# Loading v through GpSimd's DMA queue with a cast on the way, and running a fixed table of orders: a chunk-selecting attention with a gated feed-forward layer behind it

## The chip, the cores and the metric

The kernel runs on one core of a Trainium2 chip. The metric is the device time of one execution in microseconds (us); below, times without a unit are us. A core has five engines that run their own instruction streams and meet at semaphores: PE (TensorE, matrix multiplication), ACT (ScalarE), DVE (VectorE), POOL (GpSimd) and SP (SyncE, which here only issues DMA transfers). Transfers are issued by SP, ACT or POOL and carried out by the core's DMA engines.

## What is computed

The inputs are q, k and v of shape (4, 8, 768, 64), in float32, and the weights of a gated feed-forward layer. For each query, the keys are taken in chunks of 32; an upper bound of the score of each chunk is made from the chunk's minimum and maximum of k, the six best causal chunks are kept, and an ordinary softmax attention runs over them. Its result goes through an RMS norm and the gated layer.

```python
k_min = np.min(k_chunks, axis=3)
k_max = np.max(k_chunks, axis=3)
ub = np.sum(np.maximum(q[:, :, :, None, :] * k_min[:, :, None, :, :], q[:, :, :, None, :] * k_max[:, :, None, :, :]), axis=-1)
ub = np.where(causal, ub, -1000000000.0)
top_chunks = np.argsort(ub, axis=-1)[..., -top_k:]
scores = scale * np.matmul(q, k.transpose(0, 1, 3, 2))
mask = sel & (pos[:, None] >= pos[None, :])
attn = np.exp(scores)        # masked, less the row's maximum
attn = attn / (np.sum(attn, axis=-1, keepdims=True) + 1e-09)
x = np.matmul(attn, v)       # then (batch, position, head * 64): 3072 x 512
xn = x / rms * rms_g
g = xn @ w_gate              # 512 x 1536
val = xn @ w_val             # 512 x 1536
out = (g * sigmoid(g) * val) @ w_out   # 1536 x 512
```

## The kernel before, in words

The 3072 tokens are cut into twelve blocks of 256 (four batches by three blocks of the sequence), taken in the order of `ORDER` (line 501); block (b, m) is block m of batch b. A name like `scores(2, 1, 0)1` means batch 2, block 1, head group 0 (four heads of eight), against key block 1.

For each block, `load_qk` (line 586) brings k and q in float32, `load_v` (line 614) brings v in two halves of 128 tokens. `job` (line 768) transposes k and q on DVE ("turn"), makes bf16 copies of them on ACT or POOL ("half"), the chunk minima and maxima on DVE ("ext"), their difference ("dk") and operands derived from them ("bd", "KX", "relu", "qx", "qm"). `pick` (line 647) multiplies these on PE ("upper"), selects the best six on DVE and makes a mask. `unit` (line 911) is the scores on PE, followed by an exponential on ACT and, on the diagonal, a triangular cut on POOL ("tri", line 936). `values` (line 991) multiplies with `VX`, which holds v in bf16 and a column of ones behind each head, so that the softmax's denominator comes out of the same multiplication. `norm` (line 1024) makes the normalized, transposed activations `xsT`; for the last eight blocks the transposition is a DMA from SP ("across"). `ffn` (line 1099) has, per block, six pairs of units "wg" and "wv" (the two first weight matrices), tanh on ACT, "tg" on DVE, a copy "vcopy" on ACT, "hh" on POOL or DVE, and then "project" with the third weight matrix, a copy "out" and a store.

v takes this way: SP issues a load of 256 KB (128 tokens, eight heads, float32) into `vraw`, of which there are two; ACT or POOL copies a head group from there into one of the 18 rotating `VX` tiles, and this copy makes the bf16 ("vx", line 901). Each `VX` tile serves all later blocks of its batch.

The weights come in nine transfers (three each of wg, wv and wo), issued by POOL, cast to bf16 on the way; they wait for `dk(0, 0, 0)` (`GATES`, line 508). The k, q and v loads of block 2 wait for a part of wg, those of block 3 for parts of wo (`HELD`, line 584).

The order of the work is no Python loop's. Every step is recorded as an operation with its engine (or several to choose from), its cost, what it reads and writes and which buffers it takes. `Plan.run` (line 255) then simulates the engines and DMA queues (`Rings`, line 37) and picks for each engine, from what is ready, the operation with the earliest of the 1,580 due times in the table `DUE`. Where PE would stand idle before about 60 us, it puts in matmuls whose result is not used (`keep_busy`, line 1242): 77 narrow ones of 128 columns ahead of the first scores, and 39 wide ones of 512 columns in eleven places after that. What is written out is five fixed instruction streams; at run time only semaphores hold them.

## Time and profile before

| what | us |
|---|---|
| three runs | 299.69, 300.06, 302.14 |
| median | 300.06 |
| span of the profiled execution | 297.4 |
| ACT busy in it | 216.7 |
| DVE busy in it | 217.1 |
| POOL busy in it | 155.6 |

The span is the time from the first instruction to the last in one profiled execution; the device time of the runs has a few us around it. The profile gives no separate device time for the profiled execution, so its span stands beside the median of the runs, 2.66 us below it. Busy time counts neither waits nor the issue of DMA transfers. In views of the trace, a line ends with the idle time of the engine just before the instruction, and with what released it.

### The profile page before, as it was taken

Reading aid. Unit: us, or ns where it says so; the run is one execution under the profiler, and the core shown is the slowest. Engines: PE = TensorE matmul, PEld = TensorE weight load, DVE = VectorE, ACT = ScalarE, POOL = GpSimd, SP = SyncE. Lnnn points to the kernel's source line nnn. Section 1 sums busy time; section 2 is a strip of 40 time slices with the busy share of each in tenths; the row PEclk is TensorE's granted clock in tenths of the full one; section 3 lists DMA queues with packets and bytes.
Section 4 is the critical chain, followed back from the end, with each engine's and each line's share of the span. In section 5 each row is a group of like instructions: output and inputs, shape, how many; then the busy total and the mean of one; then the engine's idle time right before and its main releaser. Section 6 shows DMA issues by size and latency. Waiting matters only on the chain.

```text
span 297.4 us, 11418 instructions
## 1 busy us (share of the span) xinstructions
PE 282.5 (95%) x4672; PEld 213.4 (72%) x4672; DVE 217.1 (73%) x623; ACT 216.7 (73%) x372; POOL 155.6 (52%) x266
## 2 busy tenths in 40 slices
PE   7879999999999996999999999899999999999994
PEld 7548777657858854878767787488688778678763
DVE  6987774977998998888999999679356454456430
ACT  4897877688979876987985797677587668565331
POOL 4885858755976864475583276538044114214120
PEclk9999999999999999999999999999999999999998
DMA  7999998755676656654768576511014021011011
GB/s 188 208 204 206 255 197 163 159 130 134 141 194 154 144 136 103 149 100 110 205 135 162 108 193 150 133 40 39 0 57 55 1 82 30 2 73 35 2 71 71
DMA packets 86388, 35.08 MB, mean 118 GB/s; under 512 B 74816, under 2 KB 81728, under 8 KB 86336
## 3 DMA queue, kind: packets, MB, share of 16 engines
q1 hardware_dynamic: 80736, 29.12, 42.6%
q0 software_dynamic: 4752, 4.72, 9.4%
q8 instruction: 36, 0.59, 0.8%
q10 hardware_dynamic: 848, 0.53, 0.7%
q14 instruction: 16, 0.13, 0.2%
HBM read 28.58 MB, written 6.29 MB: 117 GB/s over the span
## 4 chain that ended last, share of the span: by engine, by line
PE 76%; DMA 9%; DVE 4%; ACT 4%; SPq 3%; POOL 1%; issue 1%; DVEq 0%; POOLq 0%; ACTq 0%
PE F L1122 39%; PE F L1169 18%; PE S L922 6%; PE F L998 6%; PE F L680 3%; SPq L528 3%; PE S L933 2%; DMA xsT<-xs 2%; DMA qraw<-in_q_dram 2%; DMA vraw<-in_v_dram 2%; DMA kraw<-in_k_dram 2%; DVE kx L809 1%; POOL hh L1144 1%; DVE m L739 1%; ACT th L1129 1%
## 5 line engine op out<-in xcount | busy, mean ns | idle before, releaser
L972 ACT ACTIVATE pt<-S 128x1024 bf16<-128x1024 f32 (+3 forms) x104 | 85.6, 857 | 19.7 <-PE S L933 18.2
L1144 POOL TENSOR_TENSOR hh<-tg,vs 128x512 bf16<-128x512 bf16 x48 | 55.7, 1164 | 42.6 <-ACT vs L1141 22.9
L1133 DVE SCALAR_TENSOR_TENSOR tg<-th,F 128x512 bf16<-128x512 bf16 x72 | 48.4, 680 | 39.3 <-ACT th L1129 33.7
L1122 PE MATMUL F<-xsT,wg 128*128 128x256 bf16 (+1 forms) x608 | 72.6, 267 | 3.7 <-DVE xnat L1017 1.7
L1122 PE MATMUL F<-xsT,wv 128*128 128x256 bf16 (+1 forms) x608 | 72.4, 267 | 0.6 <-DMA xsT<-xs 0.3
L1169 PE MATMUL F<-wo,hh 128*128 128x512 bf16 (+1 forms) x300 | 68.5, 371 | 1.8 <-POOL hh L1144 0.6
L1122 PEld LDWEIGHTS <-wg 128*128 128x128 bf16 x608 | 55.6, 98 | 13.5 <-issue 2.7
L1122 PEld LDWEIGHTS <-wv 128*128 128x128 bf16 x608 | 55.2, 98 | 9.7 <-DMA vraw<-in_v_dram 0.8
L1129 ACT ACTIVATE th<-F 128x512 bf16<-128x512 f32 x72 | 42.5, 598 | 19.7 <-PE F L1122 17.4
L942 POOL TENSOR_SCALAR_AFFINE_SELECT pt<-pt 128x512 bf16<-128x512 bf16 x48 | 32.2, 674 | 32.3 <-ACT pt L972 31.7
L1169 PEld LDWEIGHTS <-hh 128*128 128x128 bf16 x300 | 27.7, 98 | 28.4 <-issue 1.8
L1141 ACT ACTIVATE vs<-F 128x512 bf16<-128x512 f32 x48 | 28.7, 598 | 13.2 <-PE F L1122 10.1
L922 PE MATMUL S<-qb,kb 32*128 32x256 bf16 (+1 forms) x800 | 32.8, 253 | 2.3 <-ACT qb L801 2.0
L809 DVE TENSOR_REDUCE kx<-kT 128x16 f32<-128x512 f32 x48 | 30.4, 664 | 0.0
L998 PEld LDWEIGHTS <-pt 128*128 128x128 bf16 x672 | 24.8, 98 | 3.1 <-issue 0.3
L998 PE MATMUL F<-VX,pt 128*128 128x65 bf16 x672 | 26.6, 194 | 0.2 <-ACT vs L1141 0.2
L922 PEld LDWEIGHTS <-kb 32*128 32x128 bf16 x800 | 13.9, 92 | 15.0 <-issue 14.4
L933 PE MATMUL S<-mtd,chunkrow 32*128 32x128 bf16 (+2 forms) x384 | 20.5, 203 | 0.2 <-issue 0.2
L933 PE MATMUL S<-mto,chunkrow 32*128 32x128 bf16 (+2 forms) x384 | 19.9, 203 | 0.0
L1017 DVE TENSOR_TENSOR xnat<-F,rden 128x256 bf16<-128x256 f32 x48 | 19.2, 415 | 0.7
L933 PEld LDWEIGHTS <-chunkrow 32*128 32x128 bf16 x768 | 18.5, 93 | 1.2 <-issue 0.4
L1034 ACT ACTIVATE junk<-xnat 128x512 bf16<-128x512 bf16 x24 | 15.1, 631 | 5.4 <-DVE xnat L1017 5.0
(71 smaller groups left out, 337.2 us busy)
## 6 DMA issues: line engine op xcount, KB each, us to landing
vraw<-in_v_dram SPq DMA_DIRECT2D x24, 256.0 KB, 4.4
out_dram<-osb SPq DMA_DIRECT2D x23, 256.0 KB, 2.4
kraw<-in_k_dram SPq DMA_DIRECT2D x72, 64.0 KB, 2.4
qraw<-in_q_dram SPq DMA_DIRECT2D x72, 64.0 KB, 2.2
QX<-qT SPq DMA_DIRECT2D x32, 64.0 KB, 2.7
wg<-in_moe_w_gate_dram POOLq DMA_DIRECT2D x3, 512.0 KB, 12.3
wv<-in_moe_w_val_dram POOLq DMA_DIRECT2D x3, 512.0 KB, 14.3
wo<-in_moe_w_out_dram POOLq DMA_DIRECT2D x3, 512.0 KB, 23.5
```

Of the source, the lines that this page charges most:

```text
L809: plan.op(f"ext{n}{J}", "DVE", 0.585, 0.67, lambda n=n, op=op: VE.tensor_reduce(out=at(kx)[:, g, n], in_=at(kT).rearrange("p h (j c x) -> ...
L922: TE.matmul(s[a // 2][:, a % 2, c0:c0 + q1 - q0], kbt[r, t, ks], qbt[r, t, q0:q1], start=(t == 0), stop=(t == 1 and not mask), skip_group_ ...
L933: TE.matmul(o, chunkrow[r, BLK * kg + P * e:BLK * kg + P * (e + 1)], mv, start=False, stop=(d == 1), skip_group_check=True)
L942: GE.affine_select(out=d, in_=d, compare_op=ALU.is_ge, fill=0.0, base=0, pattern=[[0, 4], [1, P]], channel_multiplier=-1)
L972: lambda pt=pt, hs=hs, c0=c0, c1=c1, x=sc[hp]: SE.activation(out=at(pt)[:, hs, c0:c1], in_=at(x)[:, :, c0:c1], func=ACT.Exp, scale=SCALE), ...
L998: TE.matmul(o[:, a, :], p_[:, a, off:off + P], vt[:, e, a, :], start=(kb_ == 0 and a == 0), stop=(kb_ == nkb - 1 and a == 3), skip_group_c ...
L1122: TE.matmul(at(p_)[:, n * W:(n + 1) * W], w[:, g, ht * P:(ht + 1) * P], at(xT)[:, g, x0:x0 + W], start=(g == 0), stop=(g == NP - 1), skip_ ...
L1129: plan.op(f"tanh{U}.{hp}", "ACT", 0.48, 0.6, lambda th=th, gp=gp: SE.activation(out=at(th), in_=at(gp), func=ACT.Tanh, scale=0.5), pri - 0 ...
L1133: VE.scalar_tensor_tensor(out=at(tg), in0=at(th), scalar=1.0, in1=at(gp), op0=ALU.add, op1=ALU.mult), pri - 30, reads=[th, gp], writes=[tg ...
L1141: plan.op(f"vcopy{U}.{hp}", "ACT", 0.48, 0.6, lambda vs=vs, vp=vp: SE.activation(out=at(vs), in_=at(vp), func=ACT.Copy), pri + 0.1, reads= ...
L1144: plan.op(f"hh{U}.{hp}", "POOL", 1.11, 1.16, lambda tg=tg, vs=vs, hh=hh: GE.tensor_tensor(out=at(hh), in0=at(tg), in1=at(vs), op=ALU.mult) ...
L1169: TE.matmul(at(op)[:, cs], at(key)[:, o:o + P], wo[:, ht, cs], start=(ht == 0), stop=(ht == NHT - 1), skip_group_check=True)
```

## The change

v is now loaded by POOL instead of SP, straight from float32 in memory into bf16 in its place. There is one tile per block, `VX[b, m]`, for all eight heads, so twelve tiles that stay for the whole kernel; `vraw`, the 18 rotating tiles and the 24 copies "vx" are gone. The ones are set in twelve memsets in place of 18. A load waits for its tile's ones, and `values` waits for the loads that it needs.

```diff
-    buffers("vraw", 2, [P, 2, NG, 4, D], FP32)
-    buffers("VX", 18, [P, 2, 4, D + 1], BF16)
+    VX = {(b, m): sb.tile([P, 2, H, D + 1], BF16, name=f"VX{b}{m}") for b in range(B) for m in range(NBLK)}
...
-        for i, t in enumerate(store["VX"]):
+        for i, x in enumerate(ORDER):
...
     def load_v(i):
         b, m = ORDER[i]
-        key = ("vraw", b, m)
         for e in range(2):
             t0 = BLK * m + P * e
-            dma(f"load v{b}{m}{e}", "SP", v[b, :, t0:t0 + P, :].rearrange("a p d -> p a d"),
-                lambda e=e: at(key)[:, e].rearrange("p g a d -> p (g a) d"),
-                64, 0.023 if i < 2 else 0.019, loads_due(i, 2 if i != 1 else -1), writes=[key],
-                takes=[(key, "vraw")] if e == 0 else (),
-                behind=[HELD[i][1]] if i in HELD and e == 0 else ())
+            dma(f"load v{b}{m}{e}", "POOL", v[b, :, t0:t0 + P, :].rearrange("a p d -> p a d"),
+                lambda e=e: VX[b, m][:, e, :, 0:D], 64, 0.023, loads_due(i, 2), writes=[("VX", b, m, e)],
+                reads=[("ones", (b, m))])
...
-        flex(f"vx{J}", {
-            "POOL": (0.57, 0.62, lambda: GE.tensor_copy(vout(), vin())),
-            "ACT": (0.54, 0.63, lambda: SE.activation(out=vout(), in_=vin(), func=ACT.Copy)),
-        }, base + 4 - first, reads=[vraw] + ones, writes=[vx], takes=[(vx, "VX")])
...
-                    p_, vt = at(pts[kg]), at(("VX", b, kg, g))
+                    p_, vt = at(pts[kg]), VX[b, kg]
...
-                        TE.matmul(o[:, a, :], p_[:, a, off:off + P], vt[:, e, a, :],
+                        TE.matmul(o[:, a, :], p_[:, a, off:off + P], vt[:, e, 4 * g + a, :],
```

The second half of the change replaces the planner. `DUE`, `Rings` and the simulation in `run` are gone; a table `STEPS` names each operation (its number times eight, plus the engine) in the order in which it is written out, and a table `SLOTS` says which buffer of its pool each one takes. Negative entries are the unused matmuls.

```diff
+        seen = set()
+        for x in self.STEPS:
+            if x < 0:
+                n, slot = divmod(-x, 16)
+                fill[-1](n // 2, slot, n % 2)
+                continue
+            seq, e = divmod(x, 8)
+            o = self.ops[seq]
+            assert all(d.seq in seen for d in o.deps + o.after), o.name
+            seen.add(seq)
+            o.alts[self.ENGINES[e]][2]()
```

So the order on all engines is new, and with it some choices of engine. What the streams of the two kernels show:

| | before | after |
|---|---|---|
| transfers that SP issues | 262 | 238 |
| v loads that POOL issues | 0 | 24 |
| copies "vx" on ACT, on POOL | 10, 14 | 0, 0 |
| "relu" on POOL, on DVE | 22, 2 | 14, 10 |
| "dk" on POOL, on DVE | 19, 5 | 9, 15 |
| "half" on POOL, on ACT | 26, 22 | 22, 26 |
| operations on DVE | 426 | 450 |
| unused matmuls, narrow and wide | 77 and 39 | 103 and 34 |
| wide ones behind the first wg unit | 11 | 0 |
| changes between kinds of matmul on PE | 121 | 126 |

On POOL the first instructions are now: two memsets of ones and one of BO, the load of half of v of block (0, 0), two memsets, the making of `ident` (the identity matrix that the unused matmuls and DVE's first constants read), two memsets, the other half of (0, 0) and one of (1, 0), a memset, `half k(0, 0, 0)`, the other half of (1, 0), `dk(0, 0, 0)`, a memset, and the first transfer of wg. The eight loads of the blocks that follow stand among POOL's work from its 63rd operation (`load v201`, behind the operands "bd" of block (2, 0) and ahead of an "hh") to its 113th, and the other twelve up to its 194th of 228. On SP, the k and q loads of block (1, 0) now follow those of block (0, 0) directly. The transfers on POOL's queue share eight semaphores in turn: the ninth on the queue (the third part of wg) waits for the first (the first half of v) to have landed, and so on.

More of the change, by code (lines that the diff above doesn't have):

```diff
@@ L607, in load_qk @@
                     takes=[(key, nm + "raw")] if first else (),
-                    behind=[HELD[i][0]] if i in HELD and first else ())
+                    behind=[HELD[i]] if i in HELD and first else ())
                 first = False
@@ L664, in takes, with held @@
             return [(key, pool)] if new else []
+        def held(key):
+            return [] if new else [key]
         def bank():
@@ L1005, in job @@
             o = plan.op(f"values{J}{s}", "PE", 0.129 * nkb, 0.129 * nkb + 0.16, values, pri,
-                        reads=have + [("VX", b, x, g) for x in range(m + 1)],
+                        reads=have + [("VX", b, x, e) for x in range(m + 1) for e in range(2 if x < m else s + 1)],
                         writes=[av], takes=[(av, "F")])
@@ L1245, in keep_busy @@
             TE.matmul(store["F"][slot][:, 0:x.shape[1]], ident[:], x, start=True, stop=True)
-    for o in plan.run(in_order=("kraw", "qraw", "vraw", "kT", "qT", "kb", "qb", "QX", "VX", "xsT", "xs", "hh", "xnat"),
-                      fill=(1.6, 5.6, 60.0, 0.0565, 0.216, "F", keep_busy)):
-        o.fn()
-    kernel.plan = plan
+    plan.run(fill=(1.6, 5.6, 60.0, 0.0565, 0.216, "F", keep_busy))
 _INS = ['q', 'k', 'v', 'moe_w_gate', 'moe_w_val', 'moe_w_out', 'moe_rms_g']
```

276 lines of the change are left out of this document (33 added, 243 removed), and 230 rows, old and new, of tables (DUE, SLOTS, STEPS).

## The prediction

> **What bounds the kernel now.** I read the page first: busy shares and the chain that ended last.
>
> ```profile
> span 297.4 us, 11418 instructions
> PE 282.5 (95%) x4672; PEld 213.4 (72%) x4672; DVE 217.1 (73%) x623; ACT 216.7 (73%) x372; POOL 155.6 (52%) x266
> PE 76%; DMA 9%; DVE 4%; ACT 4%; SPq 3%; POOL 1%; issue 1%; DVEq 0%; POOLq 0%; ACTq 0%
> ```
>
> PE is the bound. The change takes no useful matmul away, so it can win only what PE loses: idle time, and matmuls whose result is not used. The busy time by stretches tells where (start and end, length, then the busy time of PE, PEld, DVE, ACT, POOL, with instructions; granted clock, DMA share, GB/s):
>
> ```profile
> 0.00:20.00 20.00, 16.00 (x271) 11.56 (x272) 16.09 (x45) 14.66 (x25) 14.63 (x56) 1.00 1.00 200
> 20.00:40.00 20.00, 18.41 (x331) 14.78 (x330) 15.68 (x47) 17.56 (x40) 14.65 (x27) 1.00 1.20 221
> 40.00:60.00 20.00, 19.96 (x306) 15.06 (x306) 13.78 (x43) 13.89 (x27) 14.12 (x23) 1.00 0.87 169
> 60.00:80.00 20.00, 18.77 (x273) 14.09 (x273) 16.32 (x50) 17.98 (x37) 12.12 (x19) 1.00 0.52 129
> ...
> 100.00:120.00 20.00, 17.41 (x346) 11.89 (x345) 17.95 (x62) 14.58 (x25) 12.33 (x19) 1.00 0.58 126
> 120.00:140.00 20.00, 19.26 (x380) 16.45 (x377) 16.63 (x51) 16.99 (x29) 12.80 (x18) 1.00 0.55 116
> ...
> 180.00:200.00 20.00, 19.13 (x408) 13.57 (x400) 15.37 (x62) 13.95 (x23) 10.59 (x17) 1.00 0.44 108
> ...
> 280.00:297.40 17.40, 13.56 (x98) 9.28 (x95) 3.86 (x6) 5.05 (x9) 3.46 (x3) 0.96 0.16 60
> ```
>
> Length less busy time is PE's idle time: 4.0 in the first 20 us, 3.8 at the end, and between them 1.59 + 0.04 + 1.23 + 2.59 + 0.74 + 0.87 = 7.06; in the stretches left out PE is busy throughout. Those 7.06 and the unused matmuls are the prize; from 200 to 280 us there is none.
>
> **The start.** The timeline of PE and the chain of waits show it.
>
> ```profile
> 1.71 6.38 PE L1245 MATMUL F<-ident 128*128 128x128 bf16 x77 [1.71 <-POOL eps L551]
> 9.15 0.29 PE L922 MATMUL S<-qb,kb 32*128 32x128 bf16 x8 [1.06 <-ACT qb L801]
> ...
> 19.37 0.29 PE L922 MATMUL S<-qb,kb 32*128 32x128 bf16 x8 [0.95 <-ACT qb L801]
> ...
> 22.27 0.37 PE L698 MATMUL F<-qT,BO 64*64 64x32 f32 x10 [0.45 <-ACT xsT L1087]
> ...
> 22.85 1.07 PE L1122 MATMUL F<-xsT,wg 128*128 128x128 bf16 x16
> ```
>
> ```profile
> 10.83 6.03 DMA qraw<-in_q_dram
> ...
> 22.92 1.00 PE F L1122 x16
> 23.92 0.22 PE S L922 x8
> ...
> 49.72 2.16 PE F L1169 x10
> ```
>
> ```profile
> L1245 PE MATMUL F<-chunkrow,ident x39: 377/379/391, 9.4 to 37.3; 128*128 128x512 bf16 x39
> ```
>
> ```profile
> L1245 PE MATMUL F<-chunkrow,ident x11: 379/379/389, 25.7 to 37.3; 128*128 128x512 bf16 x11
> ```
>
> Dense PE prices come from the chain: 2.16/10 = 0.216 for a matmul of 512 columns, 1.00/16 = 0.0625 for one of 128. The first wg unit starts at 22.9, 13.75 after the first scores (9.15); of that, 28 wide unused matmuls are 6.05 and the two waits shown 1.4. Behind it follow the other 11, 2.4 us. (The second "x" rows are all 39 of them and those behind 22.8.)
>
> **Part by part.**
>
> *ident.* POOL made it by 1.7. In the new stream a load of v (and some memsets, 0.4) stands ahead. Such an issue is not in the trace; the nearest rows are the weights', of 512 runs, where a v load has 1,024:
>
> ```profile
> L528 POOL DMA_DIRECT2D wg<-in_moe_w_gate_dram x3: 767/777/992, 9.8 to 14.2; - x3
> ```
>
> So 0.77 if runs cost nothing, 1.98 if they cost all; I take 1.2. PE then starts at 1.7 + 1.2 + 0.4 = 3.3, and the narrow matmuls take 6.38 and 26 × 0.0625 = 1.6 more: first scores at 11.3, against 9.15. To the first wg unit there are now 34 wide ones (7.3), the same work (13.75 − 6.05 − 1.4 = 6.3) and one score unit more, 0.3 by its row (0.22 and change): 24.9 to 25.2 if nothing else waits. I take 24.9, **+2.0**; bounds +1.5 and +2.8 by the price of the issue. I see no slack to hide it: PE's stream here is one piece, and unused matmuls are work like any other. What goes are the waits for ACT: ACT loses two copies "vx" and hands `half k`, `half q` and a scaling of these two blocks to POOL and DVE. And q of block (1, 0), whose landing at 16.9 stands in the chain, is issued without two v loads ahead.
>
> *Behind it.* The score unit that has moved forward: **−0.3**. No unused matmul is left behind the first wg unit: **−2.4**; this holds only if the weights are there. They are close:
>
> ```profile
> L528 POOL DMA_DIRECT2D wo<-in_moe_w_out_dram x2: 747/802/857, 20.9 to 21.8; - x2
> ...
> DMA to landing us min/median/max: 22.6/23.9/25.2
> ```
>
> The last part lands at 21.8 + 25.2 = 47.0, and the first project (the row at 49.72) needs it: 2.7 of slack. In the new stream PE reaches that place at about 49.72 + 2.0 − 0.3 − 2.4 = 49.0, which leaves 2.0. v of block (2, 0), half a MB which shared the DMA engines until then, now queues behind the weights; at the 200 GB/s and more of those stretches that gives back some 2 us. So about 4 us of cover remain. Five changes of kind more: the 0.22 of a score unit are two rounds of 0.0625 and 0.1 for going in and out, so **+0.3**.
>
> *Casts and SP.*
>
> ```profile
> L904 POOL CAST VX<-vraw 128x512 bf16<-128x512 f32 x14 | 8.5, 618 | 1.8 <-DMA vraw<-in_v_dram 1.8
> L905 ACT ACTIVATE VX<-vraw 128x512 bf16<-128x512 f32 x10 | 6.1, 631 | 0.1
> ```
>
> ```profile
> SPq L528 <- DMA vraw<-in_v_dram: 4.8, 3, 1.8
> ```
>
> ```profile
> L528 SPq DMA_DIRECT2D vraw<-in_v_dram x24: 384/580/1961, 4.1 to 187.0; - x24
> ```
>
> ```profile
> L528 SPq DMA_DIRECT2D vraw<-in_v_dram x2: 427/651/875, 11.3 to 11.8; - x2
> ...
> DMA to landing us min/median/max: 12.2/15.5/18.7
> ```
>
> ACT loses 6.1, POOL 8.5. SP loses 24 × 0.58 = 14 of issuing, and the waits of 4.8 in which it stood behind a slow v load: the second half of v of block (1, 0), issued at 11.8, landed 18.7 later, at 30.5. POOL gains 24 × 1.2 = 29 (bounds 18 and 48) and loses some relu, dk and half to DVE, so it comes to some 60% of the span, less in most stretches than DVE, which gets about 24 small operations more and was busy 18 of 20 around 110 us. Behind each v load on POOL stands an "hh" or "tri" that PE needs two or three units later; that cover is one issue, 1.2, and where it is thin PE waits.
>
> Where SP held PE, the chain says so:
>
> ```profile
> 106.00 0.94 SPq L528
> ...
> 110.23 2.06 DMA QX<-qT
> ...
> 125.74 1.32 SPq L528
> ...
> 128.59 1.74 DMA kraw<-in_k_dram
> ```
>
> The idle 2.59, 0.74 and 0.87 (100 to 140, 180 to 200) end a chain of SP issues, k loads and the transposing or crossing DMAs behind them. With 14 us off SP I let 3.2 of these 4.2 go. The 2.8 of idle in 20 to 80 us hang on ACT, POOL and DVE, whose work is reshuffled; there I let nothing go net: the thin places above cost what the casts bring. **−3.2**; bounds 0 (each stall has a successor) and −6.
>
> Sum: 2.0 − 0.3 − 2.4 + 0.3 − 3.2 = −3.6, span 293.8; with the 2.66 that the median lies above the span, **296.5**.
>
> **The DMA side, and a rule.**
>
> ```profile
> q1 hardware_dynamic: 80736, 29.12, 42.6%
> q0 software_dynamic: 4752, 4.72, 9.4%
> ```
>
> A packet of SP's queue takes 0.426 × 16 × 297.4 / 80736 = 25 ns (361 bytes on average), one of POOL's 0.094 × 16 × 297.4 / 4752 = 94 ns (993 bytes as written). A v packet is 256 bytes read and 128 written; with 64 per engine and load I take 25 ns, the row of its size, and 94 ns as the upper bound. The Trainium skill (DMA: Bandwidth & Descriptors, Specifications) says that below 512 bytes the DMA engine reads, modifies and writes. That speaks against halving the written run; v's packets were below it before, and no row here shows a 128-byte write with a cast.
>
> **The rivals.**
>
> *Slower: v's packets are dear, and the weights come late.* On POOL's queue four v loads stand ahead of the first weights: 4 × 65 = 260 packets an engine, 6.5 us at 25 ns. Every nanosecond more a packet delays all nine transfers of weights by 0.26 us. The cover is 4 us and the gain 3.6, so it decides from 7.6/0.26 = 29 ns more, 54 ns. At 70 ns the delay is 11.7, less 4: 293.8 + 7.7 + 2.66 = **304.2**; at 94 ns it would be 310. For it: POOL's row is the only one with a cast. Against: per byte that row is cheaper than SP's. The rule above would have it so, by a read for each written run; this is the mechanism it would work by.
>
> *No change: the idle time comes back elsewhere.* The new order puts "relu" and "dk" on a DVE that is busy 18 of 20, and 1.2 us of issue ahead of "hh" on POOL. If the 3.2 return as other waits, 296.5 + 3.2 = **299.7**. For it: in the chain PE's share is 76% while it is busy 95%, so its waits have close successors. Against: SP's 14 us are truly gone.
>
> *Better: the waits nearly vanish.* If of the 7.06 only 1 stays: 296.5 − 2.9 = **293.6**, and 292 if the issue of v costs 0.8 and the start moves little.
>
> **How the numbers follow.** About 1% (3 us) is what a measurement can tell from no change: the three runs lie 0.8% apart. Forecast 296.5: 0.46; better, 293: 0.12; no change: 0.22; slower: 0.20. The forecast's own range is 294 to 298.5, and a quarter of it lies above 297.06, where "faster by over 1%" ends. Faster: 0.75 × 0.46 + 0.12 + a little of the third = 0.48. Slower: the fourth, beyond 303.06 in most of its cases, and a little of the others: 0.20. Between: 0.32. The range 292 to 304 leaves out the better case's end and about half of the slower one, less than 2 in 10.
>
> **What would show it.** Right: the first scores near 11 and the first wg unit near 25 in PE's timeline; no unused matmul behind it; issues of v on POOL near 1.2 and landings of the weights no later than before (the last by 47); PE's idle time between 100 and 140 under 1; DVE and ACT no busier than before by more than a few us. Wrong: PE waiting for weights (releaser DMA of wg, wv or wo) between 25 and 50 us, which is the slower rival; or idle time behind POOL's "hh" or DVE's "relu" in the middle, which is the second. If the first wg unit starts before 23, the term of the start is wrong.

## The result, and the profile after

| | before | after |
|---|---|---|
| runs | 20 | 20 |
| median, us | 300.95 | 302.71 |
| lowest to highest | 299.29 to 302.14 | 299.38 to 305.91 |
| span of the profiled execution | 297.4 | 301.0 |

The ratio is 1.0044, with a 95% interval of 1.0025 to 1.0064 (executions that were disturbed are left out of ratios, though not out of the medians). The changed kernel is slower by about 1.3 us, where 3.6 us less were forecast. Over these runs the device time lies 1.7 to 1.8 above the span of the same execution, not 2.66: the profiled execution of the kernel before, some 299.1, stood at the fast end of its runs. So spans alone overstate the difference, and where a verdict matters below it is a ratio.

The first page of the changed kernel: span, busy time and instructions of each engine, the chain that ended last by engine, and two DMA queues (packets, MB, share of 16 engines).

```profile
span 301.0 us, 11371 instructions
PE 284.7 (95%) x4693; PEld 215.9 (72%) x4693; DVE 224.1 (74%) x649; ACT 205.9 (68%) x359; POOL 164.2 (55%) x247
...
q1 hardware_dynamic: 55776, 22.82, 32.1%
q0 software_dynamic: 29712, 7.87, 26.5%
...
PE 59%; DVE 12%; DMA 12%; SPq 6%; ACT 5%; issue 3%; POOL 1%; DVEq 0%; ACTq 0%
```

What left ACT (10.8) is there, and PE is busy 2.2 longer. But PE's part of the chain fell from 76% to 59%: with as much work for PE, the last result now hangs much more often on DVE, on transfers and on SP. The same stretches as before:

```profile
0.00:20.00 20.00, 15.15 (x241) 11.86 (x242) 11.40 (x38) 8.01 (x12) 14.13 (x34) 1.00 1.29 181
20.00:40.00 20.00, 19.07 (x360) 14.62 (x359) 17.14 (x52) 15.72 (x38) 14.07 (x28) 1.00 1.22 228
40.00:60.00 20.00, 19.64 (x309) 14.96 (x308) 17.29 (x51) 15.00 (x27) 17.40 (x30) 1.00 1.00 155
60.00:80.00 20.00, 20.00 (x287) 15.28 (x286) 17.23 (x51) 18.01 (x37) 14.95 (x22) 1.00 0.69 107
80.00:100.00 20.00, 18.93 (x334) 13.54 (x332) 18.12 (x59) 15.46 (x29) 16.19 (x23) 1.00 1.02 174
100.00:120.00 20.00, 18.36 (x379) 13.10 (x375) 19.68 (x76) 15.19 (x25) 16.10 (x22) 1.00 0.59 106
120.00:140.00 20.00, 18.16 (x336) 15.27 (x335) 17.72 (x49) 15.11 (x25) 10.91 (x15) 1.00 0.92 126
```

PE's idle time from 80 to 140 us is 1.07 + 1.64 + 1.84 = 4.55; before it was 2.59 + 0.74 = 3.33 in the same 60 us. The idle time from 100 to 140 us, which was to fall under 1, is 3.48 (3.33 before), and 1.07 ahead of it is new. DVE is busy 19.68 of 20 around 110 us, and the DMA engines, 0.55 busy before from 120 to 140, are at 0.92.

The start, in PE's timeline (start, length, instruction, and the idle time just before it):

```profile
3.61 8.32 PE L1075 MATMUL F<-ident 128*128 128x128 bf16 x103 [3.61 <-POOL ident masks.py:199]
11.87 0.29 PE L752 MATMUL S<-qb,kb 32*128 32x128 bf16 x8
...
18.14 0.43 PE L763 MATMUL S<-mto,chunkrow 32*128 32x32 bf16 x4 [1.17 <-DVE mto L593]
...
24.31 0.40 PE L908 MATMUL F<-ident,xs 128*128 128x128 bf16 x4 [0.73 <-DVE xs L896]
...
27.96 1.07 PE L952 MATMUL F<-xsT,wg 128*128 128x128 bf16 x16
```

The first wg unit starts at 27.96 instead of 22.85. Behind it no unused matmul is left, as this row of PE's source line says (count, shortest, median and longest, first and last start):

```profile
L1075 PE MATMUL F<-chunkrow,ident x34: 377/379/390, 12.1 to 26.8; 128*128 128x512 bf16 x34
```

The same view for the third weight matrix, whose first and last start are the first and the last project:

```profile
L999 PE MATMUL F<-wo,hh x300: 269/379/390, 51.6 to 297.1; 128*128 128x512 bf16 x138, 128*128 128x256 bf16 x12
```

The same row of the kernel before:

```profile
L1169 PE MATMUL F<-wo,hh x300: 270/379/390, 49.6 to 293.8; 128*128 128x512 bf16 x138, 128*128 128x256 bf16 x12
```

The first project is at 51.6 (before: 49.56, in PE's timeline), the last at 297.1 (before: 293.8). So the 3.6 us between the spans split into four: +5.1 up to the first wg unit, −3.1 from there to the first project (23.6 in place of 26.7), +1.2 from the first to the last project, and 0.4 behind that. These are the parts of one execution each; over all the runs the difference is smaller, 1.3 us by the ratio.

### The profile page after: what moved, and what is told of

It is laid out like the page before. It is cut to its first block, busy times and chain, and to the rows that moved or that the text cites. A ratio compares the mean times of both kernels' runs of the same rounds, so it can differ in the third digit from the quotient of the medians.

```text
span 301.0 us, 11371 instructions
## 1 busy us (share of the span) xinstructions
PE 284.7 (95%) x4693; PEld 215.9 (72%) x4693; DVE 224.1 (74%) x649; ACT 205.9 (68%) x359; POOL 164.2 (55%) x247
## 4 chain that ended last, share of the span: by engine, by line
PE 59%; DVE 12%; DMA 12%; SPq 6%; ACT 5%; issue 3%; POOL 1%; DVEq 0%; ACTq 0%
PE F L952 30%; PE F L999 15%; DMA kraw<-in_k_dram 6%; PE S L752 5%; PE F L828 5%; SPq L367 5%; DMA rmsg<-in_moe_rms_g_dram 2%; DMA xsT<-xs 2%; PE S L763 2%; DMA out_dram<-osb 2%; DVE tg L963 1%; DVE kx L647 1%; ACT pt L802 1%; PE F L536 1%; ACT th L959 1%
## 5 line engine op out<-in xcount | busy, mean ns | idle before, releaser
L963 DVE SCALAR_TENSOR_TENSOR tg<-th,F 128x512 bf16<-128x512 bf16 x72 | 48.4, 677 | 29.3 <-ACT th L959 26.7
L772 POOL TENSOR_SCALAR_AFFINE_SELECT pt<-pt 128x512 bf16<-128x512 bf16 x48 | 33.2, 702 | 21.3 <-ACT pt L802 21.0
L752 PE MATMUL S<-qb,kb 32*128 32x256 bf16 (+1 forms) x800 | 33.6, 253 | 1.2 <-ACT pt L802 1.2
L647 DVE TENSOR_REDUCE kx<-kT 128x16 f32<-128x512 f32 x48 | 31.1, 671 | 0.1
L828 PE MATMUL F<-VX,pt 128*128 128x65 bf16 x672 | 28.8, 194 | 1.6 <-DVE osb L1017 0.8
L828 PEld LDWEIGHTS <-pt 128*128 128x128 bf16 x672 | 26.0, 98 | 5.4 <-issue 1.3
L367 POOL DMA_DIRECT2D VX<-in_v_dram x24 | 22.5, 939 | 0.5 <-POOL VX L416 0.3
L763 PE MATMUL S<-mto,chunkrow 32*128 32x128 bf16 (+2 forms) x384 | 20.6, 203 | 1.2 <-DVE mto L593 1.2
L763 PEld LDWEIGHTS <-chunkrow 32*128 32x128 bf16 x768 | 19.4, 93 | 2.2 <-issue 1.3
L1014 ACT ACTIVATE osb<-F 128x512 f32<-128x512 f32 (+1 forms) x17 | 9.7, 577 | 16.3 <-PE F L999 14.6
## 6 DMA issues: line engine op xcount, KB each, us to landing
wv<-in_moe_w_val_dram POOLq DMA_DIRECT2D x3, 512.0 KB, 11.3
```

The costliest lines, as they stand in the source:

```text
L367: o.inst = issuer[eng].dma_start(out=dst(), in_=src)
L647: plan.op(f"ext{n}{J}", "DVE", 0.585, 0.67, lambda n=n, op=op: VE.tensor_reduce(out=at(kx)[:, g, n], in_=at(kT).rearrange("p h (j c x) -> ...
L752: TE.matmul(s[a // 2][:, a % 2, c0:c0 + q1 - q0], kbt[r, t, ks], qbt[r, t, q0:q1], start=(t == 0), stop=(t == 1 and not mask), skip_group_ ...
L763: TE.matmul(o, chunkrow[r, BLK * kg + P * e:BLK * kg + P * (e + 1)], mv, start=False, stop=(d == 1), skip_group_check=True)
L772: GE.affine_select(out=d, in_=d, compare_op=ALU.is_ge, fill=0.0, base=0, pattern=[[0, 4], [1, P]], channel_multiplier=-1)
L828: TE.matmul(o[:, a, :], p_[:, a, off:off + P], vt[:, e, 4 * g + a, :], start=(kb_ == 0 and a == 0), stop=(kb_ == nkb - 1 and a == 3), skip ...
```

## The experiments

Each ratio is against the kernel before, in runs on the same chip. Names in `move` are the kernel's own; `move` takes an operation out of the table `STEPS` and puts it elsewhere, `fill` sets the number of unused wide matmuls ahead of an operation.

### The start: is it POOL's issue, or v's transfers?

Theory A is the prediction's: ident waits behind an issue on POOL. Theory B: v's transfers delay k of block (1, 0), and DVE, in order, with it. DVE's timeline of the changed kernel suggested B:

```profile
17.14 0.71 DVE L632 STREAM_TRANSPOSE kT<-kraw 128x512 f32<-128x512 f32 x1 [1.49 <-DMA kraw<-in_k_dram]
17.88 0.44 DVE L593 STREAM_TRANSPOSE mto<-mk 64x32 bf16<-64x32 bf16 x2
```

In the kernel before, the same transposition ran at 13.0 and shows no wait:

```profile
12.97 0.71 DVE L794 STREAM_TRANSPOSE kT<-kraw 128x512 f32<-128x512 f32 x1
```

The `mto` for which PE waits 1.17 stands on DVE behind a transposition that waits for k.

**ident_first**

```diff
+    move("eps", ahead_of="load v001")
+    move("ident", ahead_of="load v001")
```

> The order of the changed kernel, with eps and ident made ahead of the first load of v on POOL. Theory A (the late ident is what costs at the start): the narrow matmuls start at 1.7 in place of 3.6, the first scores near 10.1, the first wg unit at 26.2 in place of 28.0, the time 1.8 us below the changed kernel's. Theory B (k of block (1, 0) lands late, at 17.1, because v shares the DMA engines, and DVE has its transposition ahead of a mask that PE waits for): the first scores come earlier too, but the wait of PE for mto grows from 1.2 to about 2.9, the first wg unit stays at 27.5 or later, and the time falls by 0.5 us at most.

Measured: 304.03, ratio 1.0075 (1.0046 to 1.0104). PE started at 1.82, but the wait for `mto` grew to 2.3 and the first wg unit came at 28.46. The profiled execution took 309.5, well above that median, and its clock was halved twice, for 3.4 and 6.8 us, the first time from 19 us on, behind the wait of 2.3. So the size is not to be read from the profile; that an earlier ident alone gains nothing is read from the ratio.

**v1_late**

```diff
+    for n in ("load v101", "load v100"):
+        move(n, behind="wv0")
```

> The order of the changed kernel, with the two loads of v of block (1, 0) moved on POOL from ahead of wg's first part to behind wv's first part. Theory B: k of block (1, 0) lands near 14 in place of 17.1, the wait of PE for mto (1.2) is gone, the first wg unit starts near 26.5 and the time falls by 1 to 1.5 us. Theory A: the first scores stay at 11.9, the first wg unit stays near 28, and the time stays. If v then comes too late, values of block (1, 0) wait for it, near 29 us.

Measured: 301.12, ratio 0.9994 (0.9970 to 1.0019). The wait for `mto` is gone, the first wg unit comes at 26.59, 14.5 behind the first scores (12.07) in place of 16.1. That is theory B.

**both_starts**: the two edits together.

> Both edits. A and B together: first scores near 10.1, no wait for mto, first wg unit near 25, the time 3 us below the changed kernel's. If the start is made up for later by waits for the weights, the first wg unit moves but the first project (at 51.7) moves by less than 1 us, and so does the time.

Measured: 300.82, ratio 0.9985 (0.9958 to 1.0013); first wg unit 25.86, first project 49.5. So the two moves take 2.1 off the start and 0.6% (1.8 us) off the time: what is late at the start stays late. With ident early the first scores come at 9.80, but from there to the first wg unit it is 16.1 again, as PE now waits for POOL:

```profile
13.77 0.43 PE L536 MATMUL F<-qraw,BO 64*64 64x32 f32 x16 [0.47 <-POOL mhalf L392]
...
15.81 0.43 PE L828 MATMUL F<-VX,pt 128*128 128x65 bf16 x8 [0.63 <-POOL pt L772]
```

It is the best order with v on POOL that I found, and no faster than the kernel before.

**k_first**

```diff
+    # both_starts, and
+    for n in ("load k1000", "load k1020", "load k1030", "load k1010"):
+        move(n, ahead_of="load q1000")
+    move("swap(0, 0, 0)", ahead_of="turn k(1, 0, 0)")
```

> The kernel both_starts, with the k loads of block (1, 0) ahead of its q loads on SP, and the mask's swap(0, 0, 0) ahead of the transposition of that k on DVE. Theory B: PE's wait for mto is gone, first wg unit near 24.5, the time 1 us below both_starts (299.8). Rival: PE's stream to the first wg unit is as long as its fixed unused matmuls make it, first wg unit stays at 25.9, and the time stays.

Measured: 301.61, ratio 1.0024 (0.9991 to 1.0057). The transposition of that k waits for no transfer, but it had not done so in both_starts either. DVE's wait for the first q grew from 0.80 to 1.52, and the first wg unit is at 26.53, 0.7 later. So k was no longer what held the start.

### DVE's greater load

**dve_back**: both_starts, with 13 of "relu" and "dk" given back to POOL and 6 other operations to ACT.

```diff
+    for n in ("relu(0, 1, 1)", "relu(0, 2, 0)", "relu(2, 1, 1)", "dk(0, 1, 0)", "dk(0, 1, 1)", "dk(1, 1, 0)", "dk(0, 2, 0)",
+              "dk(2, 1, 0)", "dk(1, 2, 0)", "dk(3, 1, 1)", "dk(2, 2, 0)", "dk(2, 2, 1)", "dk(3, 2, 0)"):
+        give(n, "POOL")
...
```

> The kernel both_starts, with 19 operations of blocks 4 and later given back from DVE to POOL or ACT, as the kernel before has them: 3 relu and 10 dk to POOL, 2 swap, 2 qx and 2 output copies to ACT, some 6 us off DVE between 80 and 200 us. If DVE's load makes the waits of the middle: PE's idle time from 80 to 200 us falls from 4.1 to under 3 and the time by 1 to 2 us (to 299). If they come from the place of the work in the streams or from transfers: no change, or slower by what POOL's longer dk costs.

Measured: 301.50, ratio 1.0011 (0.9984 to 1.0039). DVE's busy time fell from 223.9 to 217.2, what it was before the change, and the time did not fall; PE's idle time from 80 to 200 us stayed at 4.2 (4.05 in both_starts). The work went to POOL and ACT, so a cost there could hide a gain. But no_v, below, is as fast as the kernel before without loads although its DVE is busy 222.2, against 216.9 there. DVE's greater load alone is not the cause.

### What v costs in each order

**no_v**: in the changed kernel a memset on POOL stands in for each load of v.

```diff
-            dma(f"load v{b}{m}{e}", "POOL", v[b, :, t0:t0 + P, :].rearrange("a p d -> p a d"),
+            plan.op(f"load v{b}{m}{e}", "POOL", 0.3, 0.4, lambda e=e: GE.memset(VX[b, m][:, e, :, 0:D], 0.5),
```

> The changed kernel with each load of v replaced by a memset of the same half tile on POOL, at the same place in POOL's stream; v is left out of the computation. Theory C (v's packets on POOL's queue are dearer than on SP's, 33 ns to 19 by the shares of the queues, and slow k, q, QX and xsT transfers in the middle): idle time of PE from 80 to 200 us falls from 5.7 to under 3, k and q loads land in 2.4 in place of 3.3 us, and the time falls by 4 to 6 us with the start's part. Rival D (the new order itself, with more on DVE, makes the waits of the middle): idle time from 80 to 200 us stays at 5 or more, and the time falls by the start's 2 us at most.

Measured: 296.91, ratio 0.9834 (0.9798 to 0.9870). The time fell as theory C has it, but PE's idle time from 80 to 200 us did not: 4.18 in the profiled execution, neither under 3 (C) nor 5 and over (D).

**before_no_loads**: the kernel before without the loads; `vraw` is constant, the copies stay.

```diff
+    for t in store["vraw"]:
+        VE.memset(t[:], 0.5)
...
+            o.fn = lambda: None
```

> The kernel before without its loads of v (vraw is set once to a constant; the copies into VX stay, so v's values are left out). It says what the v loads on SP's queue cost there. The same step in the changed kernel was worth 5.8 us. If v on POOL is the dearer transport (C): 299 or more here. If v's bytes cost as much on either queue and the order is the difference (D): 295 to 297.

Measured: 296.64, ratio 0.9841 (0.9802 to 0.9880). Without v's transfers the two orders run equally fast, within the intervals. The new table by itself is worth nothing that can be measured.

**before_no_v**: neither loads nor copies; the multiplication reads a constant tile.

```diff
-                    p_, vt = at(pts[kg]), at(("VX", b, kg, g))
+                    p_, vt = at(pts[kg]), constant
```

> The kernel before with neither the v loads nor the 24 copies into VX; the multiplication reads a constant tile, so the output is not the attention's. Theory A (the copies lie beside PE's work and cost nothing): the time of the run that lacks only the loads, 296.6 us, ratio 0.982 to 0.987. Theory B (the copies on ACT and POOL hold PE up): 1 to 3 us less than that, 293.5 to 295.5, ratio 0.975 to 0.98.

Measured: 296.90, ratio 0.9885 (0.9844 to 0.9926). Taking out the 24 copies as well gains nothing more, as far as the intervals reach: they lay beside PE's work.

**before_one_head** and **after_one_head**: in each kernel the loads are issued as they are, but bring one head of eight. The other seven are constant; in after_one_head POOL sets them ahead of each load.

```diff
-            dma(f"load v{b}{m}{e}", "SP", v[b, :, t0:t0 + P, :].rearrange("a p d -> p a d"),
-                lambda e=e: at(key)[:, e].rearrange("p g a d -> p (g a) d"),
+            dma(f"load v{b}{m}{e}", "SP", v[b, 0:1, t0:t0 + P, :].rearrange("a p d -> p a d"),
+                lambda e=e: at(key)[:, e, 0, 0:1, :],
```

> The kernel before, with each v load still issued by SP but bringing one head of eight (128 packets in place of 1,024), the other heads constant. The 24 issues on SP and the 24 copies stay, so the output is not the attention's. Theory A (what v costs are its packets on the shared DMA engines): about 297 us, ratio 0.985 to 0.99, near the 296.6 of the run without v loads, and k and q land sooner between 80 and 140 us than in the kernel before. Theory B (what v costs are SP's 24 issues, 14 us of them, as the prediction's term has it): over 299 us, ratio 0.995 to 1.0.

> The changed kernel, each v load still issued by POOL but bringing one head of eight, the other seven set to a constant by POOL (some 0.5 us each), so the output is not the attention's. Theory A (v's packets are what costs): about 297 to 298, ratio 0.985 to 0.99, near the 296.9 of the changed kernel without v loads; k of block (1, 0) lands before 14 us. Theory B (the issue on POOL, 0.94 us each ahead of hh and tri, is what costs): 300 or more, ratio 0.997 to 1.005.

Measured: before_one_head 299.45, ratio 0.9954 (0.9925 to 0.9982); after_one_head 295.97, ratio 0.9866 (0.9820 to 0.9912). The two orders are opposites here. In the order of the kernel before, seven eighths of v's bytes cost 1.4 us (1 − 0.9954), and the 24 issues of SP with the remaining eighth, and what waits for their landing, another 2 to 3.4 (0.9954 less 0.9885 or 0.9841). In the changed order the 24 issues of POOL cost at most some 1 us more than the memsets of 0.55 that stand for them in no_v (0.9866 less 0.9834, which lies within the intervals), and seven eighths of the bytes 5.3 us (1.0044 − 0.9866), 3.6 of them even with the better start (0.9985 − 0.9866). The intervals leave about 1 us on either side of the 1.4 and 1.5 on either side of the 5.3, so the two are apart.

The middle of both_starts by stretches (stretch, length, busy time of PE, PEld, DVE, ACT, POOL; clock, DMA share, GB/s):

```profile
80.00:140.00 60.00, 57.26 (x1076) 43.66 (x1058) 56.98 (x183) 46.95 (x80) 43.80 (x61) 1.00 0.86 134
140.00:200.00 60.00, 58.69 (x1133) 43.35 (x1132) 53.04 (x176) 44.79 (x73) 25.51 (x37) 1.00 0.47 94
```

The same of after_one_head:

```profile
80.00:140.00 60.00, 57.90 (x1072) 44.83 (x1068) 58.37 (x187) 47.57 (x80) 45.69 (x73) 1.00 0.58 115
140.00:200.00 60.00, 59.79 (x1169) 44.23 (x1167) 53.16 (x184) 46.27 (x78) 27.42 (x42) 1.00 0.34 83
```

PE's idle time in these 120 us falls from 4.05 to 2.31 when the DMA share from 80 to 140 us falls from 0.86 to 0.58, although POOL does more. These are single executions, and no_v, with a DMA share of 0.50, has 4.18. From the first to the last project the profiled executions of the changed order with all of v and an undisturbed clock take 243.5 (both_starts) to 245.9 (v_pool_f32, below), after_one_head 241.2 and no_v 242.8. So the bytes do lengthen the middle, by some 1 to 5 us; which waits they make there, these traces don't tell apart.

### Queue, cast or order?

The price of a v packet can be worked out from the queues. For the change: 0.265 × 16 × 301.0 = 1276 us of DMA engine time on POOL's queue, less the weights' 447 (4752 × 94 ns), over 24,960 packets: 33 ns. On SP before: 0.426 × 16 × 297.4 = 2027, less 0.321 × 16 × 301.0 = 1546 for the rest, over 24,960: 19 ns. So I put the same loads into the changed order three ways, into spare tiles that nothing reads (the multiplication reads a constant), each with the two moves at the start.

```diff
-    VX = {(b, m): sb.tile([P, 2, H, D + 1], BF16, name=f"VX{b}{m}") for b in range(B) for m in range(NBLK)}
+    VX = {(b, m): constant for b in range(B) for m in range(NBLK)}
+    spare = [sb.tile([P, H, D], FP32, name=f"spare{n}") for n in range(8)]
...
-                lambda e=e: VX[b, m][:, e, :, 0:D], 64, 0.023, loads_due(i, 2), writes=[("VX", b, m, e)],
+                lambda e=e: spare[(2 * i + e) % 8][:], 64, 0.023, loads_due(i, 2), writes=[("VX", b, m, e)],
```

**v_pool_bf16**: on POOL with the cast (spare tiles in bf16).

> The control of the two: POOL issues the loads with the cast, 128 bytes written a packet, into eight spare tiles that nothing reads, the multiplication reads a constant tile. If no multiplication ever waited for v itself, the time is that of the kernel with the two moves, ratio 0.996 to 1.001, packet 33 ns. If v's landing held something up: 0.990 or less.

Measured: 301.37, ratio 0.9994 (0.9965 to 1.0022): both_starts again, so no multiplication waits for v itself, as far as the intervals reach.

**v_pool_f32**: on POOL without a cast.

> As the run with SP's loads, but POOL issues them; float32 to float32, no cast, 256 bytes written a packet. If the cast and its halved written run are dear: the packet is under 25 ns and the ratio 0.986 to 0.992. If it is POOL's queue: the packet is over 28 ns and the ratio that of the cast, within 0.003.

Measured: 302.14, ratio 1.0019 (0.9992 to 1.0045). Its own row of POOL's queue:

```profile
q0 software_dynamic: 6672, 11.01, 18.5%
```

0.185 × 16 × 299.6 = 887, less 447: 440 us for all of v, against some 810 with the cast (v_pool_bf16). The page counts 6672 − 4752 = 1,920 packets for these loads, not 24,960: without the cast a packet holds many runs. So the prices compare per run of 64 values: 18 ns in place of 33. Without the cast the engines spend half the time on v, and the kernel's time is the same or longer. So the cast, with the shorter run that it writes and its smaller packets, nearly doubles the price of v, as the prediction feared, and that is not what the time hangs on.

**v_sp_f32**: the same loads, in the same order, issued by SP.

```diff
+    for b, m in ORDER:
+        for e in range(2):
+            give(f"load v{b}{m}{e}", "SP")
```

> The changed kernel with the two moves at the start, in which all 24 v loads are issued by SP, in float32, into eight spare tiles that nothing reads; the multiplication reads a constant tile, so the output is not the attention's. With one head only, POOL's loads gave 0.9866, with all heads and the two moves 0.9985. Theory A (what eats the gain is the price of a v packet on POOL's queue): packets near 19 ns again, ratio 0.988 to 0.994. Theory B (SP's 24 issues cost as much as the dear packets): 0.996 to 1.002, with SP's issues late and PE idle between 80 and 200 us over 4.

Measured: 307.33, ratio 1.0186 (1.0149 to 1.0223). In the changed order, with each load at its place in the table, SP is the dearer issuer, by 1.7% (5 us) against POOL without a cast. PE's idle time between 80 and 200 us is 9.3 (for 3.4 of these us the clock was halved too):

```profile
80.00:140.00 60.00, 54.28 (x1028) 40.89 (x1027) 52.85 (x180) 44.67 (x77) 34.10 (x49) 1.00 0.65 149
140.00:200.00 60.00, 56.39 (x1018) 40.95 (x1015) 49.72 (x146) 42.33 (x69) 21.51 (x31) 0.97 0.47 108
```

Then the mirror image, in the order of the kernel before: only the issuing engine of later loads changes.

```diff
-            o.inst = issuer[eng].dma_start(out=dst(), in_=src)
+            o.inst = issuer[by or eng].dma_start(out=dst(), in_=src)
...
+                by="POOL" if i >= 4 else None)
```

**before_v_from4** (16 loads, none before 77 us) and **before_v_from2** (20 loads, from the third block).

> The same from the fifth block on: 16 loads on POOL, none of them before 80 us, so that the weights and the start see nothing of it. Theory A: 298.5 to 300, ratio 0.992 to 0.998. Theory B: 1.0 to 1.008.

> The kernel before in its own order, with the 20 v loads of the blocks from the third on issued by POOL instead of SP, at the place in the order where SP issued them, in float32 into vraw; the copies stay. Theory A (SP's relief is worth what the one-head run and the run without loads leave between them, some 2 to 3 us for 24 issues, and POOL's issue costs under 1): 298 to 299.5 us, ratio 0.990 to 0.996, which beats both kernels. Theory B (POOL's queue is what costs, whatever the order): 301 to 304, ratio 1.0 to 1.01, with PE waiting for POOL's hh and tri.

Measured: before_v_from4 305.39, ratio 1.0195 (1.0149 to 1.0240); before_v_from2 306.71, ratio 1.0234 (1.0205 to 1.0264). Here POOL is the dearer issuer, by 2%, beyond both ranges. POOL's timeline in before_v_from4 shows how, at one place:

```profile
141.74 1.89 POOL L528 DMA_DIRECT2D vraw<-in_v_dram  x2
...
147.41 0.93 POOL L528 DMA_DIRECT2D vraw<-in_v_dram  x1
149.97 0.61 POOL L905 CAST VX<-vraw 128x512 bf16<-128x512 f32 x1 [1.63 <-DMA vraw<-in_v_dram]
150.53 0.89 POOL L528 DMA_DIRECT2D vraw<-in_v_dram  x1
151.43 1.17 POOL L1145 TENSOR_TENSOR hh<-tg,vs 128x512 bf16<-128x512 bf16 x1
```

The same place in the kernel before:

```profile
147.29 0.62 POOL L904 CAST VX<-vraw 128x512 bf16<-128x512 f32 x1
147.87 1.16 POOL L1144 TENSOR_TENSOR hh<-tg,vs 128x512 bf16<-128x512 bf16 x1
```

POOL comes to the first two loads only when the "hh" ahead of them is done, at 141.74; SP, which has nothing but issues, sent them from 140.2 on. They land 5.3 and 7.2 us after their issue (all four of these loads: 3.5 to 4.8 before), so the copy waits 1.63 for them, and the copy and the next issue hold the next "hh": 3.6 us later than before, where the "hh" ahead (140.64 against 139.07) had been 1.6 later. How much of the 5.7 us comes about in this way was not added up.

**before_v_pool**: the planner of before, v cast on POOL, loads from the third block on behind the last weights; the order is planned anew.

```diff
+            if i > 1:
+                c, n = ORDER[i - 1]
+                o.after += [x for x in plan.ops if x.name in ("wo2", f"dk({c}, {n}, 0)")]
```

> The kernel before, with its planner, and only v changed: loaded by POOL with the cast into twelve resident tiles, no copies; from block 2 on each half waits for wo's last part and the dk of the block before. If the transport is what costs (Theory C), it is slower than the kernel before by 1 us or more, k and q loads land later than in the kernel before, and the first wg unit comes at 25 or later. If the searched order is what costs (rival D), it is at or below the kernel before, 301 or less.

Measured: 318.20, ratio 1.0532 (1.0480 to 1.0583). The planner put the start together badly: PE waits 1.88 and 3.23 before 20 us, and the clock is granted at 0.78 and 0.70 of full speed from 10 to 30 us. It says that this planner's costs don't fit such loads, and no more.

### A version to beat both

PE's start in both_starts still held waits and unused matmuls. **start_cut** moves the loads of v of block (1, 0) and `wg1` behind two triangular cuts on POOL, four operations forward on DVE, leaves out eight unused matmuls and puts the first wg unit where four of them stood.

```diff
+    # eps and ident as in ident_first, and
+    for n in ("load v101", "load v100", "wg1"):
+        move(n, behind="tri(0, 0, 1)a")
+    move("swap(0, 0, 0)", ahead_of="ubn(0, 0, 1)")
+    move("mk(0, 0, 1)", ahead_of="turn k(1, 0, 1)")
+    move("mt(0, 0, 1)", ahead_of="rden(0, 0, 0)0")
+    move("scale00", ahead_of="ext1(1, 0, 0)")
+    fill(1, "values(0, 0, 1)0")
+    fill(8, "values(0, 0, 0)1")
+    fill(0, "upper(1, 0, 1)")
+    move("wg(0, (0,)).0", ahead_of="upper(1, 0, 1)")
```

> The changed kernel with ident ahead of the first v load and the loads of v of block (1, 0) behind the two first triangular cuts on POOL; on DVE swap(0,0,0), mk(0,0,1), mt(0,0,1) and scale00 moved forward; 3 + 1 + 4 of the unused wide matmuls before the first wg unit left out, and that unit ahead of upper(1,0,1). If the late start is all that the changed order still has against it: first wg unit at 22.5 to 23.5 (25.9 with the two moves alone), first project near 47, time 298 to 299.5, ratio 0.988 to 0.994. If the time saved at the start is waited for again later (weights, DVE, DMA): 300 to 301.5, ratio 0.996 to 1.0.

Measured: 303.08, ratio 1.0093 (1.0062 to 1.0123). The stretches of its start show why (the clock is the third number from the end):

```profile
20.00:24.00 4.00, 2.00 (x32) 1.25 (x30) 2.99 (x8) 2.38 (x8) 3.09 (x9) 0.94 1.72 182
24.00:30.00 6.00, 5.60 (x102) 4.64 (x101) 2.81 (x18) 2.41 (x7) 2.95 (x5) 0.50 1.19 262
30.00:34.00 4.00, 4.00 (x79) 3.68 (x77) 2.66 (x11) 2.90 (x7) 1.74 (x3) 0.96 1.20 232
```

And PE's timeline in the same place, with its waits in brackets:

```profile
21.63 0.30 PE L828 MATMUL F<-VX,pt 128*128 128x65 bf16 x4 [1.18 <-POOL pt L772]
...
23.64 0.40 PE L828 MATMUL F<-VX,pt 128*128 128x65 bf16 x4 [0.82 <-POOL pt L772]
...
25.88 1.86 PE L952 MATMUL F<-xsT,wg 128*128 128x128 bf16 x16 [0.40 <-DVE ubn L561]
```

PE was busy 2.0 of 4 us, and then its clock was halved for 6.8 us: the first wg unit takes 1.86 in place of 1.07. Two of the eleven executions had a mean granted clock of 1.000 and 0.998: they took 301.14 and 302.22, against a median of 300.55 for the kernel before on that chip. So a full clock did not put this start ahead either. **start_warm** puts unused matmuls back where PE waited, and changes `tri(0, 0, 1)b` and `half k(1, 0, 1)` on POOL.

```diff
+    # start_cut, with
+    fill(2, "values(0, 0, 1)0")
+    fill(10, "scores(0, 0, 1)0b")
+    fill(10, "values(0, 0, 0)1")
+    fill(2, "turn(0, (0,))")
+    fill(3, "upper(1, 0, 0)")
+    move("tri(0, 0, 1)b", ahead_of="dk(1, 0, 0)")
+    move("half k(1, 0, 1)", behind="tri(0, 0, 1)b")
```

> The kernel with the cut start, but with PE kept at work: of the wide unused matmuls before the first wg unit 33 stand (2, 1, 10, 10, 2 and 3 ahead of the waits, the first five unchanged and the four behind upper(1,0,0) left out), and tri(0,0,1)b and half k(1,0,1) change places on POOL. If the halved clock after the waits was what the cut start cost: granted clock 1.00 throughout from 10 to 50 us, first wg unit at 23.5 to 25, first project near 48, ratio 0.990 to 0.996. If the start isn't what the time hangs on: 0.997 to 1.002.

Measured: 303.87, ratio 1.0074 (1.0034 to 1.0113). The first wg unit came at 25.1, but PE waited again around 23 us and the clock was halved for 3.4 us from 26 on; the first project came at 51.1. Both theories of this run failed: the cover was not complete, so this run doesn't tell what a cut start with a full clock is worth. No version with v in it beats the kernel before by more than can be measured.

## Why the prediction was wrong, point by point

Two terms of the sum failed, the start and the middle (casts and SP), and both lack the same thing: a price for v's transfers themselves on POOL's queue, beyond their issue and the delay of the weights.

**The start, +2.0: right in direction, mis-sized; it measured +5.1.** The load's issue ahead of ident was 1.09 at its longest row, ident came at 3.6 where 3.3 was forecast, and the first scores at 11.87 where 11.3 was. That part held. (The sum took the lower end of its own 24.9 to 25.2, without the score unit's 0.3, and credited the same 0.3 behind.) From there to the first wg unit the prediction took 13.6 us, "if nothing else waits"; it was 16.1. It counted the waits of the kernel before as gone, put none in their place (1.17 and 0.73 are shown), and looked at v's loads only as issues on POOL. The transfers themselves were not in the sum: with them ahead, k of block (1, 0) was turned at 17.14 in place of 13.0, and DVE's order passed that on. v1_late removes that wait and takes 1.6 of the 2.5 us that the stretch was too long; most of the rest is the 0.73 that PE waits for `xs` on DVE, which stays. That the start has no slack was right: what the moves gain at the start is gained at the end. That "unused matmuls are work like any other" was not the whole: start_cut, without eight of them, lost the full clock.

**Behind the first wg unit, −0.3 and −2.4: right.** The stretch to the first project shrank by 3.1, and no unused matmul is left in it. The weights were no obstacle: the last part was issued at 35.7, and at the 7.8 us that wo's transfers took by median it landed near 43.5, where 47 had been allowed for.

**Casts and SP, −3.2: this is the step that failed.** In the profiled executions the time between the first and the last project grew by 1.2 (with the +0.3 for changes of kind, which can't be told apart in it, −2.9 had been forecast). The step had two halves.

- *A cost of v on SP of this size is real.* In the order of the kernel before, SP's 24 issues with an eighth of the bytes cost 2 to 3.4 us, which is the size predicted; in the changed order SP as issuer costs 5 us more than POOL. The copies, though, were worth nothing (before_no_v), as far as the intervals reach.
- *That the relief would be left over was wrong.* The sum let v's transfers cost on POOL's queue what they had cost on SP's, apart from a delay of the weights. They cost 1.4 us in the old order and 5.3 in the new, where some 1.8 of it lies at the start. Nor did SP, with 24 issues less, leave the chain that ended last: its share rose from 3% to 6%. The prediction moved v's bytes into a new order and priced the order at nothing but its issues. Neither order is better in itself (296.6 and 296.9 without the loads of v); each stands only with its own issuer (v on POOL in the old one: +2%; v on SP in the new one: +1.9%).

Why the transfers cost more in the new order is only partly settled. At the start it is k of block (1, 0), as v1_late shows. In the middle it is not DVE's load (no_v), not the cast nor the price of a packet (v_pool_f32), and not that PE waits for v (v_pool_bf16). What remains, by elimination, is that they stand beside the k, q and "across" transfers on which the new order waits. From 88.7 to 98.8 us its chain of waits runs over SP and two loads of k, where the old chain ran over PE alone (start, length, what):

```profile
90.74 4.79 DMA kraw<-in_k_dram
...
95.56 3.21 DMA kraw<-in_k_dram
```

Behind that, both chains have stretches of SP and DMA. PE's longest single wait from 80 to 140 us is for a crossing transfer:

```profile
PE F L952 <- DMA xsT<-xs: 1.6, 1, 1.6
```

And the loads of k and q take longer from issue to landing (the last number, a median in us). The changed kernel:

```profile
kraw<-in_k_dram SPq DMA_DIRECT2D x72, 64.0 KB, 3.3
qraw<-in_q_dram SPq DMA_DIRECT2D x72, 64.0 KB, 3.3
```

The kernel before:

```profile
kraw<-in_k_dram SPq DMA_DIRECT2D x72, 64.0 KB, 2.4
qraw<-in_q_dram SPq DMA_DIRECT2D x72, 64.0 KB, 2.2
```

after_one_head:

```profile
kraw<-in_k_dram SPq DMA_DIRECT2D x72, 64.0 KB, 2.5
qraw<-in_q_dram SPq DMA_DIRECT2D x72, 64.0 KB, 2.4
```

So with an eighth of the bytes, at the same issues, k and q land about as early as in the kernel before: that v's transfers delay them is shown. It isn't the time that the engines spend on v's packets that does it, as v_pool_f32 has half of that and medians of 3.6 and 3.1. That these delays make the loss in the middle is argued, not shown: no_v has the early landings too and still 4.18 us of idle time there. Which transfer holds which was not taken apart.

**The rivals.** *Slower, by dear packets and late weights*: the packet rose to 33 ns, not to the 54 at which it was to decide, and the weights came early. The argument against it, that POOL's packets are cheaper per byte, holds per byte read (0.047 ns against 0.070) and not per byte written (0.095). The rule from the Trainium skill (DMA: Bandwidth & Descriptors, Specifications) is that transfers below 512 bytes are read, modified and written. It puts runs of 128 and of 256 bytes on the same side and so doesn't by itself explain 33 ns against 18; no run parts the cast, the shorter run and the size of the packet, and none shows an effect of the price on the time. *No change, the idle time comes back elsewhere*: nearest to what happened, 299.7 against a measured 302.7 by median; but it was to come back behind "relu" on DVE and "hh" on POOL, and the waits that the views show are behind k and the crossing transfers. *Better*: nothing for it.

**The offset of 2.66** was taken from one execution of the kernel before. Its own 1.7 would have put the forecast on 295.5, further off.

## What to carry to other kernels

A hand-over of transfers from one queue to another is to be priced with the bytes and the order in it, not with issues alone: run the kernel once without the transfers and once with an eighth of their bytes, and the two costs stand apart. Here each tuned order fitted the engine that issues its loads, and changing the engine alone lost 2%. An engine that also computes issues a load only when it gets there, so the load comes late where a queue that does nothing else was early.

## What the runs showed of the hardware

- PE's clock was halved after PE had been busy for only about half of 3 to 4 us with no single wait above 1.2 us (start_cut: 2.0 of 4; start_warm: 1.6 of 3). It stayed halved for 3.41, 6.83 or 10.24 us, one, two or three times the same length (these two runs, ident_first and before_v_pool; the last two have single waits of PE of 1.9 us and more as well). The Trainium skill (TensorE: Matmul & The Clock Gate, What's actually happening) gives a window of about 3.4 us, which agrees, and has the clock fall after an idle window; here a half-idle one was enough. In start_cut, the first wg unit behind it took 1.86 us in place of 1.07.
- A load of 64-value runs costs a DMA engine 33 ns a run when POOL's queue casts it to bf16, and 18 when the same queue doesn't and puts many runs into a packet (1,920 packets for all of v in place of 24,960), about as on SP's queue (19). POOL's issue takes 0.94 us with the cast and 0.93 without.
